# Moving group 0's values and the third scores, and using one x buffer, in a segment-recurrent attention kernel

## Chip, cores and metric

The kernel runs on one core of one Trainium2 chip. The metric is the time on the device of one execution, in microseconds (us). The kernel before was timed three times.

## The reference, cut to what matters

The program computes two independent attentions and puts their outputs side by side. Part A is a dilated sliding-window attention; the change leaves it alone. Part B is a recurrence over 64 segments of 32 tokens: each segment's 8 memory rows are the first 8 output rows of the segment before.

```python
B, S, Dm = (1, 2048, 640); H, Dh = (32, 192); M, seg = (8, 32)
for s in range(n_seg):                                  # n_seg = 64
    xs = x[:, s * seg_len:(s + 1) * seg_len, :].copy()
    h = jnp.concatenate([mem, xs], axis=1)              # 40 rows
    q = jnp.einsum('btd,dhe->bhte', h, Wq)
    k = jnp.einsum('btd,dhe->bhte', h, Wk)
    v = jnp.einsum('btd,dhe->bhte', h, Wv)
    scores = jnp.einsum('bhqe,bhke->bhqk', q, k) * scale
    scores = jnp.where(mask[None, None], scores, -1000000000.0)
    p = _softmax(scores, axis=-1)
    o = jnp.einsum('bhqk,bhke->bhqe', p, v)
    o = jnp.einsum('bhte,hed->btd', o, Wo)
    mem = o[:, :M, :].copy()
    outs.append(o[:, M:, :])
```

## The kernel before, in words

**Stages.** Part A and the first loads of weights come first; from about 0.17 ms on the 64 segments of part B follow one another, and a last stage multiplies the output rows that were put aside.

**One segment.** Of a segment's 40 rows, 32 (8 of memory, 24 of x) are projected in the segment itself ("main"). The last 8 x rows don't depend on the recurrence; they are projected ahead, for four segments at a time ("ahead" or late rows), and in each segment only some projections renew them: RENEW names K of group 0 and V of group 2 where s%4 = 0, k1 and v3 where it is 1, k2 and v0 where it is 2, k3 and v1 where it is 3. Such a projection has twice the matmuls and two accumulators. The late rows of Q are renewed at the end of a segment for the next one.

**Groups.** The 32 heads are worked in four groups. A weight matrix falls into pieces: five for each of q, k, v and group (384 KB each) and 24 of the output matrix "o" (320 KB each). Most pieces stay in SBUF for good (wres); those in STREAMED are fetched from a copy in HBM in every segment (wcopy), into six buffers (tile t, pool b_ws, line 427) by the SP queue, in the order in which TensorE uses them: 24 pieces in a segment.

**Engines.** TensorE (PE) runs in exactly the order of the text of segment(). The order on the other engines and on the SP queue is chosen by a list scheduler at compile time, which takes what it holds to be ready, the earlier in the text the sooner. The steps that matter:

- project32 (line 498): the projections, 20 matmuls, four side by side, with HX as the stationary side; accumulators come from a pool of three buffers (acc). to_sb (line 505) copies an accumulator, turn (line 511) transposes it on PE, fill (line 516) copies it into QT or KT, lines 528 keep late rows in Lb.
- values (line 556): ACT copies the accumulator of V into Vst, one buffer for all groups; DVE copies renewed late rows into Lv.
- scores (line 565), softmax (lines 572 to 581, DVE with one exponential on ACT, tile t1 in one buffer), put_p (line 590, tile P), turn_p (line 597 on PE, line 600 on DVE into PT).
- mix (line 613): P times V, 16 matmuls; ACT and DVE copy the halves into OT (line 618), and POOL copies the late rows of OT into OL (line 619).
- project_out (line 637) and, for group 3, project_last (line 657): OT times the output matrix, in pairs of heads; one piece a pair.
- join (lines 644, 646) and close: line 662 adds the sums and writes them as Ysb into OT; line 665 transposes them into T, a buffer shared with PT; line 666 copies the 8 memory rows into the next segment's HX; four DMAs of POOL's queue (line 668) write the output rows, one more (line 670) puts OL aside in late_o.
- load_x (line 475, SP's queue) brings the next x rows into XS, one buffer; turn_x (line 479, DVE) transposes them into HXs, two buffers used in turn.

## Time and profile before

| What | Value |
|---|---|
| median of three runs (range) | 2032.99 us (2025.99 to 2043.52) |
| the profiled execution's own time | 2030.61 us |
| its span, first to last instruction | 2028.8 us |
| granted TensorE clock, mean | 0.987 |
| busy: PE, DVE, ACT, POOL | 1799.5, 1147.2, 826.2, 489.3 us |
| DMA: bytes, share of the 16 engines by SP's queue | 647.02 MB, 89.1% |
| 62 segments, 217.0 to 1927.4 us | 27.59 us each |

A matmul's line in the timeline gives its start, its duration, the line of the kernel, what it writes and reads, how many were merged, and in square brackets how long the engine stood before it and what ended that. Sums over many such waits stand in the table of waits. Matmuls overlap, so that the next one may start some 0.07 us ahead of the end that is given for the last.

### The profile page before, as it was taken

Reading aid. Unit: us, or ns where it says so; the run is one execution under the profiler, and the core shown is the slowest. Engines: PE = TensorE matmul, PEld = TensorE weight load, DVE = VectorE, ACT = ScalarE, POOL = GpSimd, SP = SyncE. Lnnn points to the kernel's source line nnn. Section 1 sums busy time; section 2 is a strip of 40 time slices with the busy share of each in tenths; the row PEclk is TensorE's granted clock in tenths of the full one; section 3 lists DMA queues with packets and bytes.
Section 4 is the critical chain, followed back from the end, with each engine's and each line's share of the span. In section 5 each row is a group of like instructions: output and inputs, shape, how many; then the busy total and the mean of one; then the engine's idle time right before and its main releaser. Section 6 shows DMA issues by size and latency. Waiting matters only on the chain.

```text
span 2028.8 us, 95604 instructions
## 1 busy us (share of the span) xinstructions
PE 1799.5 (89%) x41224; PEld 1128.7 (56%) x41224; DVE 1147.2 (57%) x3406; ACT 826.2 (41%) x2221; POOL 489.3 (24%) x1182
## 2 busy tenths in 40 slices
PE   8998889898988888988999888898888898989978
PEld 5565555555555555555555555555555555555557
DVE  4885556555556555555655555655555555655530
ACT  3553334443444444443444443444443444443420
POOL 5101222222222222222222222222222222222210
PEclk9999999999999999999999999999999999999989
DMA  9947989999999999999999999999999999999994
GB/s 342 287 114 253 363 305 351 320 347 330 320 328 329 331 337 332 334 348 318 349 336 334 336 335 317 332 336 328 334 327 315 320 341 331 342 329 313 341 342 132
DMA packets 299048, 647.02 MB, mean 319 GB/s; under 512 B 59468, under 2 KB 88524, under 8 KB 298624
## 3 DMA queue, kind: packets, MB, share of 16 engines
q1 hardware_dynamic: 284032, 627.53, 89.1%
q0 software_dynamic: 14080, 13.04, 1.9%
q8 instruction: 323, 5.29, 1.0%
q14 instruction: 101, 0.83, 0.1%
q10 hardware_dynamic: 512, 0.33, 0.1%
HBM read 626.59 MB, written 25.62 MB: 321 GB/s over the span
## 4 chain that ended last, share of the span: by engine, by line
PE 34%; DMA 15%; DVE 4%; issue 2%; ACT 1%; POOL 1%; SPq 1%; ACTq 0%; DVEq 0%; POOLq 0%
PE acc L498 19%; DMA t<-wcopy_o 5%; DMA t<-wcopy_k 5%; DMA t<-wcopy_v 4%; PE Y L637 4%; PE px L613 3%; PE px L565 2%; PE px L511 2%; PE px L752 1%; POOL OL L619 1%; PE px L597 1%; PE acc L752 1%; DVE T L665 1%; DVE OT L662 1%; ACT Vst L556 1%
## 5 line engine op out<-in xcount | busy, mean ns | idle before, releaser
L498 PEld LDWEIGHTS <-HX 128*32 128x32 bf16 x19380 | 474.4, 97 | 384.4 <-issue 91.0
L505 ACT CAST sb<-acc 128x384 bf16<-128x384 f32 x511 | 242.1, 479 | 341.6 <-PE acc L498 321.6
L498 PE MATMUL acc<-wres_q,HX 128*32 128x384 bf16 x6460 | 326.4, 330 | 59.3 <-DVE HX L666 52.9
L498 PE MATMUL acc<-t,HX 128*32 128x384 bf16 x4848 | 319.9, 329 | 41.3 <-DMA t<-wcopy_k 19.9
L619 POOL COPY OL<-OT 128x96 bf16<-128x96 bf16 x256 | 165.4, 646 | 651.5 <-DVE OT L618 394.3
L498 PE MATMUL acc<-wres_v,HX 128*32 128x384 bf16 x4844 | 268.5, 330 | 1.3 <-issue 1.3
L498 PE MATMUL acc<-wres_k,HX 128*32 128x384 bf16 x3228 | 212.7, 328 | 1.7 <-issue 1.1
L516 POOL COPY QT<-Lb 128x96 bf16<-128x96 bf16 x252 | 67.5, 268 | 595.5 <-PE px L565 471.3
L556 ACT CAST Vst<-acc 128x384 bf16<-128x384 f32 x256 | 122.7, 479 | 209.5 <-PE acc L498 208.9
L516 DVE CAST KT<-px 128x384 bf16<-128x384 f32 (+1 forms) x242 | 116.9, 494 | 145.5 <-PE px L511 139.2
L637 PE MATMUL Y<-wres_o,OT 128*32 128x320 bf16 x2816 | 184.8, 304 | 1.8 <-DMA wres_o<-in_B_Wo_dram 1.6
L572 DVE SCALAR_TENSOR_TENSOR t<-px,mask 128x160 f32<-128x160 f32 x256 | 82.9, 324 | 156.6 <-PE px L565 154.4
L511 PE MATMUL px<-ident,sb 128*128 128x128 bf16 x1938 | 166.8, 222 | 2.5 <-issue 1.1
L613 PE MATMUL px<-PT,Vst 64*128 64x80 bf16 (+1 forms) x2048 | 122.1, 212 | 50.0 <-ACT Vst L556 28.0
L618 ACT CAST OT<-px 128x240 bf16<-128x240 f32 x256 | 92.0, 359 | 169.8 <-PE px L613 152.3
L578 ACT ACTIVATE t<-t 128x160 f32<-128x160 f32 x256 | 87.3, 341 | 161.0 <-DVE t L577 161.0
L565 PEld LDWEIGHTS <-QT 64*64 64x64 bf16 (+1 forms) x4096 | 105.3, 109 | 82.9 <-issue 73.9
L505 DVE CAST sb<-acc 128x384 bf16<-128x384 f32 x135 | 75.2, 558 | 129.1 <-PE acc L498 126.9
L580 DVE TENSOR_REDUCE sm<-t 128x4 f32<-128x160 f32 x256 | 81.9, 320 | 110.9 <-ACT t L578 107.5
L637 PE MATMUL Y<-t,OT 128*32 128x320 bf16 x1792 | 128.9, 303 | 15.8 <-DMA t<-wcopy_o 14.3
L511 PEld LDWEIGHTS <-sb 128*128 128x128 bf16 x1938 | 109.6, 98 | 57.4 <-issue 41.9
L613 PEld LDWEIGHTS <-Vst 64*128 64x128 bf16 (+1 forms) x2048 | 64.5, 98 | 138.3 <-ACT Vst L556 57.7
(94 smaller groups left out, 2569.3 us busy)
## 6 DMA issues: line engine op xcount, KB each, us to landing
t<-wcopy_k SPq DMA_DIRECT2D x640, 384.0 KB, 5.6
t<-wcopy_o SPq DMA_DIRECT2D x603, 320.0 KB, 4.7
t<-wcopy_v SPq DMA_DIRECT2D x320, 384.0 KB, 4.8
wres_q<-in_B_Wq_dram SPq DMA_DIRECT2D x20, 384.0 KB, 8.2
late_o<-OL POOLq DMA_DIRECT2D x64, 96.0 KB, 5.5
wres_q<-late_o SPq DMA_DIRECT2D x16, 384.0 KB, 6.1
wres_v<-in_B_Wv_dram SPq DMA_DIRECT2D x15, 384.0 KB, 9.6
XS<-xwindows SPq DMA_DIRECT2D x64, 80.0 KB, 5.6
```

The source lines that it names most:

```text
L498: nc.tensor.matmul(ps[n][32 * j:32 * j + 32, :], lhsT=X[:, dc, :], rhs=w[:, 384 * j:384 * j + 384], start=(dc == 0), stop=(dc == 4), tile_ ...
L505: copy(sb[:], p[:])
L511: nc.tensor.matmul(pt[:, c], lhsT=sb[:, 128 * c:128 * c + 128], rhs=ident, start=True, stop=True)
L516: copy(t[:, :, :, n0:n1], src)
L556: copy(t[:], p[:])
L565: nc.tensor.matmul(Sps[64 * h:64 * h + 64, a, :], lhsT=QT[k0:k1, at:at + 64], rhs=KT[k0:k1, c, a, :], start=(outer == 0 and a == 0), stop= ...
L572: nc.vector.scalar_tensor_tensor(out=t1[:], in0=Sps, scalar=scale, in1=mask[:].unsqueeze(1).to_broadcast([128, 4, L]), op0=ALU.mult, op1=A ...
L578: nc.scalar.activation(t1[:], t1[:], ACTF.Exp)
L613: nc.tensor.matmul(ps[r][lo:hi, 2 * L * k:2 * L * k + 2 * L], lhsT=V[64 * r:64 * r + 64, col:col + hi - lo], rhs=PT[64 * r:64 * r + 64, 2 ...
L618: copy(OT[:, 6 * r:6 * r + 6].rearrange("p c n -> p (c n)"), ps[r][:, 0:6 * L])
L619: nc.gpsimd.tensor_copy(OL[:, :, 12 * g:12 * g + 12].rearrange("p n c -> p c n"), OT[:, :, 32:L])
L637: nc.tensor.matmul(Y[t:t + 32].rearrange("p (b c) -> p b c", b=2), lhsT=OT[:, slot(c), 0:32], rhs=wide(w, r, gv), start=(i == 0), stop=(i ...
```

## The change

It does five things:

1. values(s, 0) moves from in front of mix(0) to behind the projections of Q and K of group 2, ahead of scores(1). values(s, 1) moves ahead of mix(0), and since Vst is one buffer its copies wait until mix(0) has been written down: values now returns the copying as a function, keep.
2. scores(2) and its softmax move to right behind mix(0); project_out(Y, 0) is split around turn_p(1).
3. Ysb and T go into the two halves of XS, no longer into OT and PT's buffer.
4. HX is one buffer. turn_x(s + 1) comes behind values(s, 3), and load_x(s + 1) from the start of the segment to behind values(s, 0).
5. STREAMED names other pieces: 14 of q, k, v and 10 of o, where there were 15 and 9.

```diff
-STREAMED = {"q": ((), (), (), ()), "k": ((0, 1), (1, 2, 3), (0, 1, 3), (2, 3)), "v": ((0, 4), (1,), (4,), (3,)),
-            "o": (3, 5, 7, 8, 11, 13, 16, 20, 21)}
+STREAMED = {"q": ((), (), (), ()), "k": ((3, 4), (1, 4), (0, 2), (0, 2)), "v": ((4,), (0, 3), (0, 3), (2,)),
+            "o": (1, 3, 7, 10, 11, 15, 17, 18, 22, 23)}
...
-    HXs = [xpool.tile([128, 2, 5, SEG], BF16, name=f"HX{i}") for i in range(2)]
+    HX = xpool.tile([128, 2, 5, SEG], BF16, name="HX")
...
-        for t, p, copy in ((LV[g], ps[0], ENGINES["LV"][g]), (Vst, ps[-1], ENGINES["V"][g]))[0 if renew else 1:]:
-            copy(t[:], p[:])
+        def keep():
+            for t, p, copy in ((LV[g], ps[0], ENGINES["LV"][g]), (Vst, ps[-1], ENGINES["V"][g]))[0 if renew else 1:]:
+                copy(t[:], p[:])
+
+        return keep
...
-        Ysb = OT[:, 0:4].rearrange("p c n -> p (c n)")
+        Ysb, T = XS[:, 0:160], XS[:, 160:320]
         nc.vector.tensor_tensor(Ysb, Y, part, op=ALU.add)
         if s + 1 < n_seg:
-            T = one.tile([128, 4, 2, L], BF16, tag="PT", name="T")[:].rearrange("p a b n -> p (a b n)")[:, 0:160]
             nc.vector.transpose(T, Ysb.rearrange("p (f k) -> p k f", k=5))
-            nc.vector.tensor_copy(HXs[(s + 1) % 2][:, 0, :, 0:M], T.rearrange("p (k n) -> p k n", n=SEG)[:, :, 0:M])
+            nc.vector.tensor_copy(HX[:, 0, :, 0:M], T.rearrange("p (k n) -> p k n", n=SEG)[:, :, 0:M])
...
     def segment(s):
         last = s + 1 == n_seg
-        load_x(s + 1)
...
         tk[2] = project_qk(s, "k", 2)
+        values(s, 0)()
+        load_x(s + 1)
         soft = softmax(scores(1))
         tq[2]()
         tk[2]()
         PT[0] = turn_p(0)
         put_p(s, 1, *soft)
-        values(s, 0)
+        v1 = values(s, 1)
         mix(0, PT[0])
-        values(s, 1)
+        v1()
+        soft = softmax(scores(2))
+        Y = ps_y.tile([128, 320], FP32, tag="y")
+        project_out(Y, 0, range(0, 4))
         PT[1] = turn_p(1)
-        Y = ps_y.tile([128, 320], FP32, tag="y")
-        project_out(Y, 0)
-        put_p(s, 2, *softmax(scores(2)))
+        project_out(Y, 0, range(4, 6))
+        put_p(s, 2, *soft)
...
         mix(2, PT[2])
+        values(s, 3)()
         turn_x(s + 1)
-        values(s, 3)
```

More of the change, by code (lines that the diff above doesn't have):

```diff
@@ L478, in turn_x @@
         if s < n_seg:
-            nc.vector.transpose(HXs[s % 2][:], XS[:].rearrange("p (w f k) -> p w k f", w=2, k=5))
-    def main(s):
-        return HXs[s % 2][:, 0]
-    def ahead(s):
-        return HXs[s % 2][:, 1]
+            nc.vector.transpose(HX[:], XS[:].rearrange("p (w f k) -> p w k f", w=2, k=5))
+    main, ahead = HX[:, 0], HX[:, 1]
     def bank():
@@ L533, in project_qk @@
         renew = s == 0 or f"{m}{g}" in RENEW[s % 4]
-        Xs = [ahead(s), main(s)] if renew else [main(s)]
+        Xs = [ahead, main] if renew else [main]
         ps = project32(Xs, m, g)
@@ L553, in values @@
         renew = s == 0 or f"v{g}" in RENEW[s % 4]
-        ps = project32([ahead(s), main(s)] if renew else [main(s)], "v", g)
-        for t, p, copy in ((LV[g], ps[0], ENGINES["LV"][g]), (Vst, ps[-1], ENGINES["V"][g]))[0 if renew else 1:]:
-            copy(t[:], p[:])
+        ps = project32([ahead, main] if renew else [main], "v", g)
+        def keep():
+            for t, p, copy in ((LV[g], ps[0], ENGINES["LV"][g]), (Vst, ps[-1], ENGINES["V"][g]))[0 if renew else 1:]:
+                copy(t[:], p[:])
+        return keep
     def scores(g):
@@ L701, in segment @@
         mix(1, PT[1])
-        values(s, 2)
+        values(s, 2)()
         tq[3]()
@@ L718, in segment @@
             gl = (s + 1) % 4
-            ql = project32([ahead(s + 1)], "q", gl)
+            ql = project32([ahead], "q", gl)
             sb = to_sb(ql[0], S_)
```

## The prediction, made before the changed kernel was run

> **What bounds the kernel now.** I read the page first, then the windows, then who kept TensorE (PE) waiting, then one segment of the recurrence as a timeline. On the page PE is busy nine tenths nearly everywhere, and so are the 16 DMA engines; the windows say it for the middle of the run.

> ```profile
> PE 1799.5 (89%) x41224; PEld 1128.7 (56%) x41224; DVE 1147.2 (57%) x3406; ACT 826.2 (41%) x2221; POOL 489.3 (24%) x1182
> ...
> DMA  9947989999999999999999999999999999999994
> ```
> ```profile
> core 0: us, PE busy (x) PEld busy (x) DVE busy (x) ACT busy (x) POOL busy (x), PEclk, DMA share, GB/s
> 900.00:1200.00 300.00, 268.94 (x6440) 165.76 (x6435) 175.10 (x563) 126.52 (x348) 75.87 (x186) 0.99 0.95 335
> ```
> The reader is to see two resources near full side by side: PE busy 268.94 of 300 us, DMA 0.95 at 335 GB/s. A gain on one is kept only if the other can follow. The copies of line 666, one at the end of each segment but the last, run from 217.0 to 1927.4 us: 62 segments of 27.59 us. PE's waits in that stretch:

> ```profile
> engine line waited for: us in total, times, longest us
> PE acc L498 <- DVE HX L666: 52.1, 62, 1.1
> PE px L613 <- ACT Vst L556: 26.8, 46, 0.6
> PE px L613 <- DVE PT L600: 21.5, 65, 0.7
> PE acc L498 <- DMA t<-wcopy_k: 18.7, 35, 2.2
> PE acc L498 <- DMA t<-wcopy_v: 18.0, 30, 2.5
> PE Y L637 <- DMA t<-wcopy_o: 10.6, 23, 1.4
> ...
> PE px L613 <- DVE Lv L556: 8.4, 16, 0.5
> ```
> Three places matter: the end of a segment (HX, 0.84 us each), the first mix (Vst or Lv, once in every segment), and streamed weights (18.7 + 18.0 + 10.6 and 4.7 at line 657: 52 us, 0.84 us a segment).

> **Part 1: group 0's values moved ahead.** An ordinary segment, number 29, with PE first, then ACT, then DVE:
> ```profile
> 997.57 0.34 PE L498 MATMUL acc<-t,HX 128*32 128x384 bf16 x4
> 998.49 0.25 PE L613 MATMUL px<-PT,Vst 64*128 64x80 bf16 x4 [0.58 <-ACT Vst L556]
> ```
> ```profile
> 997.96 0.48 ACT L556 CAST Vst<-acc 128x384 bf16<-128x384 f32 x1 [0.70 <-PE acc L498]
> ```
> ```profile
> 997.61 0.48 DVE L600 TENSOR_TENSOR PT<-px,own 128x320 bf16<-128x320 f32 x1
> ```
> PE ends the values at 997.91 and stands 0.58 us until ACT has copied them. After the change group 1's values fill the same place between turn_p(0) and mix(0), and group 0's copy is long done. Then PT is late next: it ends at 998.09, and with 0.05 us for the signal PE stands 998.14 - 997.91 = 0.23 us. Gain 0.35 us. So in segments with s%4 = 0 or 1 (32 of 64). With s%4 = 3 group 1's values are renewed, 40 matmuls in place of 20 (0.82 us more: five fours side by side, 0.164 us from start to start), which covers PT: gain 0.58 us, 16 times.

> With s%4 = 2 (segment 30) it goes against the change, for there K of group 2 and the values of group 0 are both renewed:
> ```profile
> 1021.63 0.56 DVE L505 CAST sb<-acc 128x384 bf16<-128x384 f32 x1 [0.45 <-PE acc L498]
> 1022.25 0.32 DVE L572 SCALAR_TENSOR_TENSOR t<-px,mask 128x160 f32<-128x160 f32 x1
> ...
> 1024.88 0.46 DVE L600 TENSOR_TENSOR PT<-px,own 128x320 bf16<-128x320 f32 x1
> ```
> ```profile
> 1025.39 0.25 PE L613 MATMUL px<-PT,Vst 64*128 64x80 bf16 x4 [0.73 <-DVE PT L600]
> 1026.16 0.24 PE L613 MATMUL px<-PT,Lv 64*128 64x80 bf16 x4 [0.52 <-DVE Lv L556]
> ```
> VectorE (DVE) has a queue of softmax, KT and Lb work, so PT comes 3.67 us after the scores start at 1021.67. PE gets to mix(0) at 1025.39 - 0.73 = 1024.66 today, 0.82 us earlier with the shorter values 1, and the Lv copy (0.55 us) now comes ahead of line 572, some 0.1 us later. PE waits 0.73 + 0.82 + 0.1 = 1.65 us where it waited 0.73 + 0.52 = 1.25: loss 0.40. Besides, the accumulator pool has three buffers: Q 2 takes one, K 2 two, and values 0 wants two at once right behind them. Its second waits for the DVE copy that ends at 1022.19; PE ended K 2 at 1021.74 and does 0.16 us in its first buffer: 0.3 us, with the signal about 0.35. Loss 0.75 us, 16 times (bounds 0 and 1.5: DVE taking PT first, or one more DVE copy in front).

> Sum of part 1: 32 x 0.35 + 16 x 0.58 - 16 x 0.75 = 11.2 + 9.3 - 12.0 = **8.5 us gained**.

> **Part 2: third scores behind mix(0).** The scores (16 matmuls, 0.47 us to the next start) move from behind project_out(0) to in front of it, no instruction more. What hid the OT copy, values 1 and turn_p(1), was 0.93 + 0.2 us; now only the scores do. In segment 29 mix ends at 999.00 and ACT's half is copied by 999.10 + 0.36 = 999.46, where the scores would end at about 999.47: with the signal 0.07 us, 64 times, **4.5 us lost**. The DVE half serves the fourth pair on, 0.46 us later. The gain, softmax 2 begun earlier, is worth nothing: in the waits P (line 590) stands with 5.5 us in 29, all found at turn_p(3) in the segments I followed, and turn_p(3) isn't moved. PT for mix(1) keeps 2 us of group 3's projections ahead of it.

> **Part 3: the end of a segment.** Line 662 no longer writes into OT, which POOL's line 619 reads:
> ```profile
> 1039.20 0.64 POOL L619 COPY OL<-OT 128x96 bf16<-128x96 bf16 x1 [2.13 <-DVE OT L618]
> ```
> ```profile
> 1039.87 0.33 DVE L662 TENSOR_TENSOR OT<-px,part 128x160 bf16<-128x160 f32 x1 [0.81 <-POOL OL L619]
> ```
> ```profile
> 1039.29 0.45 PE L657 MATMUL px<-wres_o,OT 128*32 128x160 bf16 x16
> ```
> The wait named is 55.8 us in all, but PE's own last product ends at 1039.74, so line 662 starts at about 1039.80 instead of 1039.87. Late next is the product itself, and HX's 0.84 us stays but for 0.07: 63 x 0.07 = **4.4 us gained**. T leaves PT's buffer, where nothing waited for it.

> **Part 4: one HX and XS.** turn_x (530 ns on DVE) must now wait for values 3. In segment 29 these end at 1009.05 and turn_x ran at 1009.41, in 30 the gap is 0.9 us: nothing. The load of XS (480 ns on SP, 80 KB) moves from late in the segment before to after values 0, and must wait until the four output DMAs have read XS. What is queued behind it on SP are the next weight fetches, and SP does stand at a fetch whose buffer isn't free (742 us in its own waits, on line 498). Output DMAs take 505 ns each on POOL and land late:
> ```profile
> 1040.14 0.55 POOL L670 DMA_DIRECT2D late_o<-OL  x1 [0.30 <-POOL OL L619]
> 1040.68 2.14 POOL L668 DMA_DIRECT2D out_dram<-OT  x4
> ```
> ```profile
> DMA to landing us min/median/max: 3.6/4.9/7.0
> ```
> The last is issued about 1042.3 and lands 4.9 us on, near 1047.2, 6.4 us into the segment of 27. XS isn't needed for another 15 us. If the load stands in SP's queue behind the fetches of that time, nobody waits (0). If it stands right behind the fetch of values 0, which takes the buffer that K 0's first streamed piece frees at about 1.5 us, SP stands 4.9 us, and the pieces of values 1, needed at about 9.8 us, are issued at 6.4 and land by the rows' 3.5 to 5.6 us at 10 to 12: up to 1.1 us a segment, 70 us. Today's SP shows that this queue's order isn't the order of the source: the XS load went out at 1037.55, behind four fetches that are written after it. I take 0, nearer to that row, and keep 70 as the far end. [...]

> **Part 5: streamed pieces.** Per segment 15 x 384 + 9 x 320 = 8640 KB become 14 x 384 + 10 x 320 = 8576 KB, 24 issues as before. That is 0.7% less, and the segment is to be 0.13 us (0.5%) shorter, so the rate asked of DMA stays and I leave its 52 us of waits where they are. Ends: the new places catch all of it (-52) or double it (+52). The last stage reads one o piece more in three passes, 0.98 MB; at the 267 GB/s of 1928 to 2012 us that is 3.7 us of transfer, mostly beside matmuls: **1 us lost**.

> **Sum.** -8.5 + 4.5 - 4.4 + 1 = -7.4 us. The profiled execution took 2030.6 us (span 2028.8), so 2023; the median of the three runs is 2.4 us above it, so **2025 us**.

> **Rivals.**
> 1. Transfers are the bound: DMA already stands at 0.95. Then time goes with bytes: 64 x 64 KB = 4.2 MB at 335 GB/s is 12.5 us, **2020**. Against it: PE's DMA waits are only 52 of 1710 us. It differs little from the sum. [...]
> 2. Both give way: DVE serves PT in time with s%4 = 2 (12 + 1.25 x 16 = 32 us better at most, half of it taken: 16) and the new places save a third of the DMA waits (17): **1992**. For it: PE's stalls in one segment stand away from the DMA waits. Against it: DVE's queue there is 3 us of work that the change leaves.
> 3. The other side: SP stands behind the XS load until the output rows are out. It decides once the load is ahead of the first fetch of values 1; one place later, SP stands some 2.5 us, and about a third of the price falls due. **2050 to 2095, say 2065.** For it: landing at 6.4 us against a queue that works only six buffers ahead. Against it: today's XS load was put where its buffer had just come free.
> 4. The DVE backlog with s%4 = 2 is worse (16 x 0.75 more) and waits for weights grow by a tenth: +17, **2042**.

> **How the numbers follow.** About 1% (20 us: under 2013, over 2053) is what a measurement of this kernel can tell from no change; the three runs alone span 17.5 us. Chances: sum and rival 1 together 0.42, rival 2 0.25, rival 3 0.23, rival 4 0.10. Faster by over 1%: rival 2 and a little of the sum's own low end, 0.28. Slower by over 1%: rival 3 and some of rival 4, 0.28. Within 1%: 0.44. The likeliest case has 2008 to 2042 for itself; the range that leaves out no more than 2 in 10 reaches from half of rival 2's way, 1998, to rival 3's 2068.

> **What would show it.** Right: the Vst wait at line 613 is gone, a PT wait near 0.23 us stands in its place with s%4 = 0 and 1 and one of about 1.6 with s%4 = 2; a wait of line 498 on the sb copy appears there; HX still costs near 0.77 us a segment; OT appears in front of line 637 with under 0.1. Wrong: HX's wait falls below 0.5 us (then POOL was the cause after all), SP's line 475 waits for DMA out_dram by several us a segment and PE's weight waits double (rival 3), or these fall by half (rival 2).

## The result and the profile after

The changed kernel takes 2124.59 us (median of four runs, 2111.99 to 2131.19) against 2029.49 us for the kernel before on the same chip (four runs by now, 2024.00 to 2043.52): ratio 1.045, 95% interval 1.038 to 1.052. It is slower by 4.5%, and the prediction of 2025 us with its range up to 2068 was wrong. Its profiled execution took 2124.67 us, its span is 2122.8 us, 94.0 us more than before; 91.7 of them lie between the first and the last copy of memory rows into HX (these end at 218.8 and 2020.9 us). By the pages, PE's busy time grew by 35 us with the same 41224 matmuls (1799.5 to 1834.4), and the rest of the span, in which PE stands, by 59 (229.3 to 288.4).

The page and the window of the same 300 us as before say first that neither resource is fuller. PE busy is down to 260 us of 300 and DMA to 0.91 at 316 GB/s (before: 0.95 at 335), and SP's queue q1 has 85.1% of the DMA engines' time (89.1% before). Something keeps both waiting.

```profile
DMA  9957989898889888899899889988989898888994
...
q1 hardware_dynamic: 284464, 624.31, 85.1%
```
```profile
900.00:1200.00 300.00, 260.37 (x6118) 159.46 (x6118) 166.98 (x531) 121.08 (x333) 72.58 (x177) 0.98 0.91 316
```

What PE waited for in the segments (waiter, line, what ended the wait; us in total, times, longest):

```profile
PE acc L494 <- DMA t<-wcopy_v: 52.2, 71, 3.4
PE acc L494 <- DVE HX L665: 46.7, 62, 0.8
PE Y L637 <- DMA t<-wcopy_o: 34.6, 55, 2.1
PE px L613 <- DVE PT L600: 33.3, 61, 2.0
PE Y L637 <- ACT OT L618: 30.8, 62, 0.6
PE px L657 <- DMA t<-wcopy_o: 19.5, 36, 1.4
PE acc L494 <- DVE sb L501: 5.4, 16, 0.3
PE acc L494 <- DMA t<-wcopy_k: 5.1, 13, 0.9
```

The Vst wait is gone, as meant. Waits for weights rose from 52 to 111 us, and a wait for OT of half a microsecond a segment is new. SP's own waits name the cause of the first:

```profile
SPq L427 <- PE acc L494: 520.6, 589, 16.0
SPq L427 <- PE Y L637: 238.2, 265, 3.8
SPq L475 <- DMA out_dram<-XS: 215.7, 87, 6.6
```

SP stood 215.7 us at the XS load until the output rows had left XS; before, all its waits at that line came to 17 us. One segment (it begins at 1147.3 us) shows it, SP first, then POOL:

```profile
1149.08 1.15 SPq L427 DMA_DIRECT2D t<-wcopy_v  x2
1154.01 0.32 SPq L475 DMA_DIRECT2D XS<-xwindows  x1
1154.42 0.88 SPq L427 DMA_DIRECT2D t<-wcopy_v  x1
1155.40 0.88 SPq L427 DMA_DIRECT2D t<-wcopy_o  x2
```
```profile
1147.30 2.01 POOL L667 DMA_DIRECT2D out_dram<-XS  x4
```

Two fetches of V go out by 1150.2; then SP issues nothing for 3.8 us, until the last of four output DMAs has landed, 6.7 us after the first was issued. The next V piece is used at 1158.07, 0.52 us late. Meanwhile DMA works off what was issued: its share is 0.97 in these 3.8 us and 0.62 in the next 4.0, and such dips lower the mean share.

**The clock.** The mean granted TensorE clock fell from 0.987 to 0.966: (1 - 0.966) x 2122.8 = 72 us of clock lost against 26. It isn't spread evenly. Around one late V piece, PE's timeline and then three windows (the third number from the end is the granted clock):

```profile
1130.71 0.35 PE L494 MATMUL acc<-t,HX 128*32 128x384 bf16 x4 [2.22 <-DMA t<-wcopy_v]
...
1132.53 0.46 PE L637 MATMUL Y<-wres_o,OT 128*32 128x320 bf16 x4 [0.51 <-ACT OT L618]
1132.77 0.48 PE L637 MATMUL Y<-t,OT 128*32 128x320 bf16 x4
```
```profile
1128.50:1132.00 3.50, 1.29 (x40) 0.79 (x39) 1.28 (x5) 0.60 (x2) 0.00 (x0) 1.00 1.01 387
1132.00:1135.40 3.40, 2.89 (x40) 1.35 (x42) 2.15 (x9) 0.81 (x3) 1.14 (x3) 0.50 0.83 291
1135.40:1138.80 3.40, 3.40 (x90) 1.92 (x80) 1.23 (x5) 1.32 (x3) 0.64 (x1) 0.99 0.83 281
```

After a stretch in which PE was busy 1.29 of 3.5 us, the clock stands at half for 3.4 us and fours of matmuls that take 0.31 us at full clock (line 637 at 1160.04) take 0.48. The trace of the kernel before has 12 such spells of half clock, 55 us; the changed kernel has 33, 146 us. That goes with the 35 us by which PE's busy time rose. A stop of PE that brings such a spell is thus paid twice.

### The profile page after: what moved, and what is told of

It is laid out like the page before. It is cut to its first block, busy times and chain, and to the rows that moved or that the text cites. A ratio compares the mean times of both kernels' runs of the same rounds, so it can differ in the third digit from the quotient of the medians.

```text
span 2122.8 us, 95612 instructions
## 1 busy us (share of the span) xinstructions
PE 1834.4 (86%) x41224; PEld 1146.6 (54%) x41224; DVE 1153.1 (54%) x3406; ACT 832.3 (39%) x2221; POOL 489.1 (23%) x1182
## 3 DMA queue, kind: packets, MB, share of 16 engines
q1 hardware_dynamic: 284464, 624.31, 85.1%
## 5 line engine op out<-in xcount | busy, mean ns | idle before, releaser
L494 PEld LDWEIGHTS <-HX 128*32 128x32 bf16 x19380 | 493.4, 99 | 415.7 <-issue 110.0
L494 PE MATMUL acc<-t,HX 128*32 128x384 bf16 x4520 | 338.1, 333 | 60.9 <-DMA t<-wcopy_v 52.7
L494 PE MATMUL acc<-wres_q,HX 128*32 128x384 bf16 x6460 | 341.6, 343 | 49.0 <-DVE HX L665 47.5
L619 POOL COPY OL<-OT 128x96 bf16<-128x96 bf16 x256 | 164.9, 644 | 576.4 <-DVE OT L618 436.2
L494 PE MATMUL acc<-wres_k,HX 128*32 128x384 bf16 x3876 | 240.1, 332 | 0.3 <-DVE sb L501 0.3
L637 PE MATMUL Y<-wres_o,OT 128*32 128x320 bf16 x2816 | 184.8, 322 | 34.1 <-ACT OT L618 31.9
L637 PEld LDWEIGHTS <-OT 128*32 128x32 bf16 x4608 | 106.2, 97 | 143.8 <-issue 64.8
L637 PE MATMUL Y<-t,OT 128*32 128x320 bf16 x1792 | 139.3, 317 | 38.4 <-DMA t<-wcopy_o 37.3
L618 DVE CAST OT<-px 128x240 bf16<-128x240 f32 x256 | 103.9, 406 | 105.7 <-PE px L613 100.8
L613 PE MATMUL px<-PT,Vst 64*128 64x80 bf16 (+1 forms) x2048 | 122.6, 213 | 34.3 <-DVE PT L600 33.3
L600 DVE TENSOR_TENSOR PT<-px,own 128x320 bf16<-128x320 f32 x256 | 122.6, 479 | 51.9 <-PE px L597 51.4
L618 ACT CAST OT<-px 128x240 bf16<-128x240 f32 x256 | 92.4, 361 | 136.6 <-PE px L613 130.0
L572 DVE SCALAR_TENSOR_TENSOR t<-px,mask 128x160 f32<-128x160 f32 x256 | 82.7, 323 | 108.7 <-PE px L565 102.9
```

What stands on the lines that cost most here:

```text
L494: nc.tensor.matmul(ps[n][32 * j:32 * j + 32, :], lhsT=X[:, dc, :], rhs=w[:, 384 * j:384 * j + 384], start=(dc == 0), stop=(dc == 4), tile_ ...
L600: nc.vector.tensor_tensor(PT[:], pt.rearrange("p l (h n) -> p (l h) n", h=2)[:, :, 0:L].unsqueeze(2) .to_broadcast([128, 4, 2, L]), own[:] ...
L613: nc.tensor.matmul(ps[r][lo:hi, 2 * L * k:2 * L * k + 2 * L], lhsT=V[64 * r:64 * r + 64, col:col + hi - lo], rhs=PT[64 * r:64 * r + 64, 2 ...
L618: copy(OT[:, 6 * r:6 * r + 6].rearrange("p c n -> p (c n)"), ps[r][:, 0:6 * L])
L619: nc.gpsimd.tensor_copy(OL[:, :, 12 * g:12 * g + 12].rearrange("p n c -> p c n"), OT[:, :, 32:L])
L637: nc.tensor.matmul(Y[t:t + 32].rearrange("p (b c) -> p b c", b=2), lhsT=OT[:, slot(c), 0:32], rhs=wide(w, r, gv), start=(i == 0), stop=(i ...
```

## The experiments

The expectations call "queue theory" the reading given above: SP stands at the XS load, the weight fetches behind it come late, and PE's long stops halve its clock. Their "rival one" is PE's new order and their "rival two" the new choice of pieces, as causes of the loss; they are not the rivals of the prediction.

"Weights" is the sum of PE's waits for streamed weights at the lines of the segments (projections, project_out, project_last), "SP at XS" SP's waits at line 475 and "lost" span times one minus the mean clock, all over the whole profiled execution (us). The ratio is to the kernel before on the same chip. The profiled execution is often the fastest of its row (2032.2 us in e1, 2080.0 in e8), so that the median run may have lost somewhat more than these columns say.

| Run | median us | ratio (95%) | weights | SP at XS | lost |
|---|---|---|---|---|---|
| before | 2029.5 | 1 | 57 | 17 | 26 |
| changed | 2124.6 | 1.045 (1.038 to 1.052) | 115 | 225 | 72 |
| e1 sums in OT | 2044.1 | 1.008 (1.005 to 1.012) | 52 | 31 | 30 |
| e2 only sums in XS | 2242.8 | 1.109 (1.102 to 1.116) | 43 | 245 | 153 |
| e4 e1 + mix's order | 2035.0 | 1.004 (1.000 to 1.007) | 53 | 32 | 34 |
| e5 changed, old pieces | 2254.6 | 1.114 (1.107 to 1.121) | 202 | 241 | 130 |
| e6 load later | 2078.0 | 1.024 (1.022 to 1.026) | 80 | 152 | 48 |
| e6c load behind mix(0) | 2078.6 | 1.024 (1.020 to 1.028) | 78 | 147 | 56 |
| e7 e4 + turn_p(0) early | 2011.5 | 0.991 (0.987 to 0.994) | 60 | 28 | 28 |
| e8 e4, old pieces | 2095.6 | 1.031 (1.026 to 1.037) | 90 | 47 | 35 |
| e9 e7, close as before | 2021.3 | 0.996 (0.992 to 0.999) | 73 | 28 | 24 |
| e10 pieces, old order | 2071.6 | 1.023 (1.017 to 1.029) | 95 | 94 | 27 |
| e11 only the order | 2104.1 | 1.038 (1.033 to 1.043) | 87 | 13 | 61 |

**e1: the end sums back in OT.** Nothing else of the changed kernel is touched.

```diff
-        Ysb, T = XS[:, 0:160], XS[:, 160:320]
+        Ysb, T = OT[:, 0:4].rearrange("p c n -> p (c n)"), XS[:, 160:320]
```

> The changed kernel with one part undone: the end sums (Ysb) go into OT again, T stays in XS, so that the XS load waits for DVE's last copy alone and no longer for the output DMAs. Queue theory (SP stands at the XS load until the output rows are out, weights come late, and PE's long stops bring half-clock spells): SP's wait of 215.7 us for out_dram is gone, PE's waits for weights fall from about 126 to 50 to 65 us, the mean granted clock goes back from 0.966 to 0.98 or more, and the time is 2030 to 2050 us; what is left over the kernel before is the OT wait of 32 us less the gains at mix(0). Rival one (PE's new order, the OT wait and the backlog with s%4 = 2, makes the loss): 2100 us or more. Rival two (the new choice of streamed pieces makes it): 2100 us or more, weights waits unchanged.

Measured 2044.1 us. The out_dram wait is gone from SP's list, weights waits are 52 us, the clock is 0.985:

```profile
SPq L475 <- DVE HX L665: 29.6, 54, 0.9
```

That is 80 us of the 95 with one line, and order and pieces are out as the main cause. The load itself stands even earlier in SP's queue here, ahead of all fetches of values; it waits for DVE's copy only, about half a microsecond at a time.

**e2: the sums in XS, alone, in the kernel before.**

```diff
-        Ysb = OT[:, 0:4].rearrange("p c n -> p (c n)")
+        Ysb, T = XS[:, 0:160], XS[:, 160:320]
...
-            T = one.tile([128, 4, 2, L], BF16, tag="PT", name="T")[:].rearrange("p a b n -> p (a b n)")[:, 0:160]
```

> The kernel before with one part of the change alone: Ysb and T in XS; order, pieces and both HX buffers as before. Queue theory: the XS load, written at the segment's start, now has to wait for the output DMAs as well; SP stands some 3 us a segment for out_dram, PE's weights waits at least double (over 100 us) and the time is 2060 to 2120 us. Both rivals: within 10 us of the kernel before, 2020 to 2040 us.

Measured 2242.8 us: the direction as expected, the size missed by more than 100 us, and weights waits didn't grow at all. SP's wait for out_dram is there (236.2 us), but with two HX buffers DVE's turn_x stands early in the queue and now waits for the late XS rows, with the softmax behind it; ACT then stands at the exponential (line 578; 161.0 us before), with the copies of accumulators for PE behind that. From DVE's, ACT's and PE's waits:

```profile
DVE HX L479 <- DMA XS<-xwindows: 174.1, 62, 5.9
```
```profile
ACT t L578 <- DVE t L577: 371.7, 142, 6.1
```
```profile
PE px L511 <- ACT sb L505: 112.7, 64, 3.8
```

So the same late load blocks a second queue here, and e2 doesn't show what SP's standing costs by itself. In the changed kernel turn_x stands behind values 3, and this second block doesn't arise.

**e5: the changed kernel with the old pieces.** STREAMED as in the kernel before.

> The changed kernel with the streamed pieces of the kernel before (15 and 9). Queue theory: SP's wait for out_dram stays near 200 us and the time stays 2100 to 2150 us. Rival one (order): likewise 2100 us or more. Rival two (pieces): PE's weights waits fall back to about 55 us and the time to 2040 us or less.

Measured 2254.6 us, 100 us above what the queue theory expected. SP's wait is as long (234 us for out_dram), but the piece next in the queue is the first of values 0, used right behind K 2; weights waits rise to 202 us. The new pieces don't make the loss: they soften it. In e2 the load has the same place (behind four fetches of K, ahead of three of V) and SP stands as long, yet weights waits are 43 us: the old order uses values 0 only behind scores(1). What standing costs depends on how soon the piece behind it is used.

**e6 and e6c: the same load at other places of SP's queue.** e6 writes load_x behind mix(1). e6c writes it behind mix(0), after a copy that it must follow:

```diff
         mix(0, PT[0])
         v1()
+        if s + 1 < n_seg:
+            nc.gpsimd.tensor_copy(XS[:, 0:1], OT[:, 0, 0:1])
+        load_x(s + 1)
```

> The changed kernel with load_x written behind mix(1): the same waits and buffers, but on SP's queue the XS load stands one to two weight fetches later. Queue theory, by place: SP still meets the load before the output rows have landed, but fewer and later-needed pieces stand behind it: SP's wait for out_dram 80 to 180 us, the time between the changed kernel and the run with the sums in OT, 2050 to 2110 us. If the place within the queue didn't matter (the load itself, or the shared buffer, costs): 2115 us or more.

> The changed kernel with the XS load put off: it is written behind mix(0), and a copy of one column of OT into XS on POOL ahead of it (overwritten by the load) makes it follow mix(0); sums stay in XS, HX stays one buffer, pieces and PE's order are the changed kernel's. On SP's queue the load now stands some seven fetches later than in the changed kernel. Queue theory: SP's wait for out_dram under 15 us, weights waits of PE 45 to 70 us, clock 0.98 or more, time 2030 to 2060 us as with the sums in OT. If the shared buffer costs in another way: 2090 us or more.

e6 came as expected: 2078.0 us, 143 us of waits for out_dram; but its load moved in half the segments only (32 times two fetches later, 30 times not at all). e6c missed. Its wait for out_dram is gone, yet it takes 2078.6 us, for SP now stands at the same line for the new copy:

```profile
SPq L475 <- POOL XS L695: 146.3, 63, 3.7
```

The miss says more than the hit would have: two different reasons to wait, of nearly equal length (152 and 147 us at the XS load), cost the same 34 us over e1. That fits the reading that SP's standing costs, whatever it stands for; different pieces stand behind the load in the two runs, so the equal size is in part chance. From 31 to 225 us of standing the time rises by 80 us.

**e4: mix takes the late rows first.** Of the changed kernel's 31.9 us for OT (30.8 in the segments) the trace shows the reason in ACT's order, in the segment above:

```profile
1159.10 0.48 ACT L554 CAST Vst<-acc 128x384 bf16<-128x384 f32 x1 [0.38 <-PE px L613]
1159.47 0.36 ACT L618 CAST OT<-px 128x240 bf16<-128x240 f32 x1
```

Group 1's values go into Vst ahead of OT, for the last matmul that reads Vst isn't the last of the mix. On top of e1:

```diff
-        plan = [(late, h, 0) for late in range(2) for h in range(2)] + [(late, h, 1) for late in range(2) for h in range(2)]
+        plan = [(late, h, middle) for middle in range(2) for late in (1, 0) for h in range(2)]
```

> The changed kernel with Ysb in OT as in the run above, and with mix taking the late rows before Vst, so that Vst's last reader is the last matmul and ACT copies OT ahead of group 1's values. Queue theory: the OT wait of 31.9 us at line 637 falls to under 8 us and the time is 25 us under that of the run above, 2000 to 2025 us, below the kernel before. Rival one (order): the OT part comes back, the rest stays, 2070 us or more. Rival two (pieces): 2070 us or more.

Measured 2035.0 us, 9 us under e1 where 25 were expected, and over the expected 2000 to 2025. The OT wait fell from 33.4 to 4.3 us, so the mechanism is right, but most of the gain didn't reach the end. Where it went is only partly seen. The sum of 4.3 leaves out 52 stands of 0.15 us for OT that are too short for the table of waits, 7.7 us in all. And with s%4 = 3 the first 16 matmuls of line 637 take 1.15 us in the median in place of 0.78, as DVE's half of OT now comes last.

**e7: turn_p(0) ahead of scores(1).** On top of e4:

```diff
         values(s, 0)()
+        PT[0] = turn_p(0)
         load_x(s + 1)
...
-        PT[0] = turn_p(0)
```

> The run with both repairs (sums in OT, mix taking late rows first), with turn_p(0) moved up behind group 0's values, ahead of scores(1), so that DVE makes PT ahead of the second softmax. My account of mix(0): the PT wait of 38 us falls to about 12 us (what mix(3) has), the waits of some 1.5 us with s%4 = 2 go, and with them the half-clock spells there; 2000 to 2020 us, under the kernel before. If transfers bound the kernel by now, PE's weights waits grow by what PT's lose, and the time stays 2025 to 2040 us.

Measured 2011.5 us: 0.9% under the kernel before (interval 0.6 to 1.3%), 5% under the changed one. PT's wait fell from 38.4 to 7.8 us, and with it the half-clock spells that e4 has behind that wait where s%4 = 2 (27 us of half clock there in e4's trace, none in e7's). PE's waits:

```profile
PE Y L637 <- DMA t<-wcopy_o: 30.5, 47, 1.5
PE px L657 <- DMA t<-wcopy_o: 16.3, 31, 1.2
...
PE px L613 <- DVE PT L600: 7.8, 39, 0.2
```

**e8, e10, e11: order and pieces apart.** e8 is e4 with the old STREAMED. e10 is the kernel before with the new STREAMED and one HX (turn_x behind values 3), order and close as before. e11 is the kernel before with the new order of segment() alone.

> The run with both repairs, with the streamed pieces of the kernel before. Part 5 of the prediction left the choice of pieces at nothing. If so also where SP isn't held up: 2025 to 2050 us. If the new pieces carry a gain of their own in the new order: 2055 us or more. If the old ones were better: under 2025 us.

> The kernel before with the new pieces and one HX (turn_x behind values 3), with its own order and its own close (part 5 and half of part 4 alone). If the pieces are fitted to the new order: weights waits grow to 60 to 90 us and the time is 2030 to 2060 us. If the new pieces are better in any order: under 2020 us. If one HX costs by itself, a wait of line 498 or 479 on the other appears.

> The kernel before with parts 1 and 2 alone (the order of the changed kernel; pieces, close, load_x and both HX as before). The prediction's sum of these parts is 8.5 gained and 4.5 lost, 2025 us. By the runs since, OT costs 32 us instead of 4.5, and the old pieces don't suit the new order: 2060 to 2100 us.

e8 2095.6, e10 2071.6, e11 2104.1 us: e8 is in its second case, pieces with a gain of their own; e10 is over the range for "fitted to the new order", and e11 is 4 us over its own. The new order with the old pieces costs 3 to 4% (e8, e11); with the new ones and SP free it stands at 1.004 (e4). The new pieces thus carry about 60 us in the new order (e8 against e4). Without them PE waits for weights at values 0: in e11, 50 of the 54 us of this row lie there (the OT wait takes another 33):

```profile
PE acc L498 <- DMA t<-wcopy_v: 54.3, 73, 2.6
```

e10 isn't clean: with one HX, SP also stood at the XS load for turn_x (89 us), so it doesn't say what the pieces alone cost.

**e9: T out of XS too.** e7 with T in PT's buffer.

> The fastest run so far (sums in OT, late rows first in mix, turn_p(0) early) with T in PT's buffer again as in the kernel before, so that XS holds nothing but the landing rows and SP waits for nothing of the segment's end. By the queue theory SP's 27 us of waits for the HX copy at the XS load go and weights waits fall by some 5 to 10 us: 2000 to 2010 us. If a short wait of 0.4 us a segment is covered by the six buffers: no change, 2008 to 2015 us.

Measured 2021.3 us, over both expected ranges, interval 0.992 to 0.999 of the kernel before; it was timed on another occasion than e7, and the two intervals overlap. SP's standing is as long as in e7, now for turn_x (19 us), and no gain shows.

## Why the prediction was wrong, point by point

- **Part 4 (one HX and XS) failed: the wait of the XS load on SP's queue was put at nothing.** It took 0 between 0 and 70 us, "nearer to that row", the place of the XS load in the kernel before. That row showed a load whose buffer comes free with a DVE instruction. The step's own figure, output rows landing 6.4 us into the segment, was right (6.7 in the segment above; 215.7 us of waits, 3.4 us a segment), and rival 3 described what came. The order at compile time put the load behind the first fetch of values in 16 segments and behind the second in 46, ahead of the rows' landing (in the segment above SP came to it 2.9 us into the segment); what the scheduler assumed of the landing, no run shows. Measured: 80 us, e1 against the changed kernel. Rival 3 expected 2.5 us of standing behind the second fetch and a third of the price; there SP stood 3.8 us in the mean. Its 70 us also lacked the half clock: (1 - 0.985) x 2030.4 = 30 us lost in e1 against 72. And 70 wasn't the far end of the prediction's own figures: pieces that land at 10 to 12 us and are needed at 9.8 come up to 2.2 us late, 141 us over 64 segments.
- **The landing**, 4.9 us in the median of the kernel before (3.6 to 7.0), stayed near that: the output DMAs take 5.2 us in the median in the changed kernel (4.0 to 6.8), while DMA moves 303 GB/s in the mean.
- **Part 2 (third scores)** was mis-sized: 4.5 us for OT, measured 30.8. The row gave ACT's copy of OT right behind the mix; it didn't ask what else becomes ready for ACT at that moment, and values 1's copy, which the change itself put there, went first (0.48 us).
- **Part 1 (values 0)** held in its terms. With s%4 = 2 PE waits 1.63 or 1.64 us for PT in 12 of 16 segments (predicted 1.65), and 0.34 us for the accumulator (0.35). The Vst and Lv waits of 35 us are gone. What it lacked is the price behind a stop of 1.5 to 1.6 us: of e4's spells of half clock inside the segments, eight of nine follow directly on a window of 3.4 us that holds that very wait. With s%4 = 0 or 1 the 0.23 us for PT show only where weights are in time.
- **Part 3 (end of a segment)** was right: HX 0.84 us before, 0.75 after. Line 662 waits for PE's last product now, and POOL was never the cause to more than 0.1 us.
- **Part 5 (pieces)** was left at nothing because the rate asked for stays. That argued from a mean; what counts is which piece is used when. In the new order the new set is worth about 60 us, and the new order by itself costs 3.8% (e11), which the sum of parts 1 and 2 (4 us gained) had missed.
- **Rivals 1, 2 and 4** are out: DMA share fell, neither PT nor weights waits shrank, PT's wait with s%4 = 2 was no worse than summed, and weights waits doubled where rival 4 had a tenth more.

## What to carry to other kernels

When a change makes a transfer wait for another one, ask on which queue it stands and what is behind it: a load that nobody needs for some 16 us (SP issues it at 1154.01 in the segment above, turn_x reads it at 1170.42) cost 80 us because weight fetches stood behind it. A buffer shared between an incoming and an outgoing transfer tied two queues together here (SP stood 215.7 us for the output DMAs of POOL's queue); when the place of a transfer in a queue is fixed at compile time, take from the trace when what it waits for has landed. And choose the order of work and the prefetched pieces together: here the new order with the old pieces lost 3 to 4%, and with the new pieces, unblocked and with turn_p(0) moved, it gained 0.9%.

## What the runs showed of the hardware that was not expected

Single stops of 1.5 to 2.2 us were often followed by 3.4 us in which TensorE's granted clock was 0.50 (behind PT's wait of 1.54 us in e4, in 8 of the 16 segments that have it), in spells of 3.41 us or a multiple: 55 us of them before, 146 in the changed kernel, 311 in e2.

PE was idle throughout in none of the windows ahead of the 35 spells that begin inside the segments of these two: it was busy for 0.48 to 2.18 us of the 3.41, in 33 of them for 0.96 us or more.
